# Fewer PE instructions, long fp32 dummies and moved value casts in the head of a linear-attention plus feed-forward kernel

## The chip, the cores and the metric

The kernel runs on one core of a Trainium2 chip. The metric is the device time of one execution in microseconds (us). "Before" is the kernel as it stood, "changed" the kernel with the diff below.

Engine names in the profile: PE is TensorE's matmuls, PEld its weight loads, DVE VectorE, ACT ScalarE, POOL GpSimd, SP the queue that issues most transfers. A "look" is the one profiled execution of a kernel; its times in us count from its first instruction.

## The reference, cut to what matters

```
q, k, v: (8 batches, 8 heads, 576 rows, 64)  f32
q_s = softmax of q over the last axis
k_s = softmax of k over the rows
kv  = k_s^T v            (64 x 64 per head)
x   = q_s kv             -> (4608, 512)
h   = x @ w_in           (512 x 2048)
g   = h * sigmoid(beta * h)
out = g @ w_out          (2048 x 512)
```

## The kernel before: the parts that the change and the argument touch

Heads go in four pairs per batch. In the head of the program (batch 0) each pair of queries is exponentiated, normalised and transposed. The keys are exponentiated, and `kv` is their product with a bf16 copy of the values. The sum over the keys is the product with a column of ones. Then `out_now` multiplies the scaled `kv` with the transposed queries, and a copy from PSUM gives `XT`, the input of the first big product. `WARM` matmuls are dummies.

```
def warm(n, bk):                              # dummies: 512 columns, bf16
    for _ in range(n):
        mm(PS[bk][:, :], WARM[:, 0:128], WARM[:, :], True, True, ...)

def ksum(b, hp, kb):                          # 9 matmuls of one column
    for j in range(NG):
        mm(PS[kb][:, hp:hp + 1], keys, ones, j == 0, j == NG - 1, ...)

def kv_mm(b, hp, bk, n):                      # 9 matmuls of 64 columns
    for j in range(NG):
        mm(PS[bk][:, VW*n : VW*n + D], keys, values[:, 0:D], ...)
...
warm(13, 0) ... warm(6, 0) ... warm(3, 0)     # between the transposes
cast_v(0, 0); cast_v(0, 1, DVE); cast_v(0, 2) # values to bf16; default is POOL
for m in range(NM): cast_win(0, m, 1, POOL)   # w_in, chunk 1
cast_win(1, 0, 2, POOL)                       # w_in, chunk 2, first half
...
ksum(0, 0, kb); ksum(0, 1, kb); ksum_inv(0, kb, 0, 2)
go(t_steps(0, (3,), (1,)))
warm(1, 0); cast_v(0, 3, ACTE)
...
at = first_tiles(0, FIRST[0])                 # hidden tiles 1 and 2
kv_mm(0, 0, 3, 0); kv_mm(0, 1, 3, 1); kvd(0, 0, 3, 0, 2)
ksum(0, 2, kb); ksum(0, 3, kb); warm(1, 0); ksum_inv(0, kb, 2, 2)
beta = read_beta()
kv_mm(0, 2, 5, 0)
out_now(0, 0, 4, ACTE)                        # 1st output product, XT copy on ACT
kv_mm(0, 3, 5, 1)
out_now(0, 1, 6, ACTE)
kvd(0, 2, 5, 0, 2); next(beta); next(beta)
at(0)                                         # first w_in matmuls
out_now(0, 2, 7, DVE); out_now(0, 3, 3, ACTE)
...
cast_win(1, 2, 2, DVE); next(beta)
for m in range(1, NM): at(m)
for c in range(2, len(WCH)):                  # chunks 3, 4, 5 of w_in
    for m in range(NM): cast_win(c, m, 1, DVE)
```

The loads are issued in one queue in this order, and none up to the last chunk of `w_in` waits for an engine: q, k, v of batch 0 (3.3 MB), then `w_in` in chunks of 256, 256, 512, 512 and 512 columns (0.5, 0.5, 1, 1 and 1 MB). Then come `w_out` (4 MB), as staging buffers come free, and q, k, v of batch 1. Hidden tiles 1 to 4 need the first two chunks, tiles 5 to 8 the third, tiles 9 to 12 the fourth. "The fifth tile" below is the first that needs the third chunk, and "PE's head" is all that PE does before it.

The softmax here doesn't subtract the row's maximum and nothing guards it: scores larger than these inputs give would overflow.

## Time and profile before

The time is 287.42 us (median of 3 executions).

| kernel before, one execution | |
|---|---|
| span | 285.5 us |
| PE busy | 278.9 us (98%) |
| third chunk of w_in landed | 19.06 us |
| PE's head ready for the fifth tile | 18.97 us (its last matmul starts at 18.76, one takes 0.216) |
| fifth tile starts | 19.57 us |
| first w_out matmul | 30.30 us |

PE is nearly full over the span. The windows view of the first 20 us shows another bound there. Columns are the stretch, its length, busy time and instruction count of PE, PEld, DVE, ACT and POOL, then the granted clock, the DMA share and GB/s:

```profile
0.00:10.00 10.00, 8.80 (x38) 3.78 (x38) 5.34 (x12) 6.65 (x11) 7.59 (x18) 1.00 0.82 286
10.00:15.00 5.00, 4.27 (x86) 3.30 (x87) 4.05 (x13) 3.67 (x5) 2.85 (x6) 1.00 1.06 373
15.00:20.00 5.00, 4.34 (x20) 1.63 (x18) 2.54 (x9) 4.25 (x8) 0.70 (x2) 1.00 1.05 386
```

From 10 us on the DMA share stays at 1.05 or above, with 373 and 386 GB/s, while every engine has idle time. The chain of work that ended last, in order of time (start, length, what; issue pieces under 0.1 us left out), passes through a transfer:

```profile
8.18 10.88 DMA WST<-in_moe_w_in_dram
19.08 0.44 DVE WIN L572
19.57 20.82 PE PS L363 x94
```

That is the third chunk, cast by DVE, after which PE starts. PE's own timeline (start, length, engine and line, operation, count, and in brackets the idle time before it and what ended it) says how near PE's head was to being the bound:

```profile
13.29 0.43 PE L363 MATMUL PS<-VB,EK 128*128 128x64 bf16 x9
13.56 0.38 PE L363 MATMUL PS<-QT,KVD 128*128 128x512 bf16 x1
13.77 0.43 PE L363 MATMUL PS<-VB,EK 128*128 128x64 bf16 x9
14.05 0.38 PE L363 MATMUL PS<-QT,KVD 128*128 128x512 bf16 x1
14.70 0.59 PE L363 MATMUL PS<-XT,WIN 128*128 128x512 bf16 x2 [0.28 <-POOL WIN L572]
15.13 0.59 PE L363 MATMUL PS<-QT,KVD 128*128 128x512 bf16 x2
15.56 0.59 PE L363 MATMUL PS<-XT,WIN 128*128 128x512 bf16 x2
16.39 2.75 PE L363 MATMUL PS<-XT,WIN 128*128 128x512 bf16 x12 [0.23 <-DVE XT L521]
19.57 10.89 PE L363 MATMUL PS<-XT,WIN 128*128 128x512 bf16 x48 [0.43 <-DVE WIN L572]
```

The sixteen matmuls of tiles 1 to 4 were done 0.43 us before the fifth tile could start. (The view counts the end of a matmul with its drain; by start times the gap is 0.6 us.)

### The profile page before, as it was taken

The page shows a single profiled execution, that of the slowest core. Times are in us where ns is not written, and L with a number is a line of the kernel's source. Part 1 is how long each engine was busy: PE and PEld are TensorE (multiplying, and loading weights), DVE is VectorE, ACT ScalarE, POOL GpSimd, SP SyncE. Part 2 cuts the span into 40 slices and gives each one's busy share as a digit, 9 for nine tenths or more (in the row PEclk, how much of TensorE's full clock was granted, in tenths as well). Part 3 has the DMA queues.
Part 4 walks back from the last instruction along what each step waited for, and adds up shares of the span by engine and source line. Part 5 has one row for each costly group of instructions (what it writes and reads, how often), then busy time and mean ns, then how long its engine had stood idle before and what let it go on. Part 6 is the DMA issues. An engine that isn't in the chain of part 4 may idle for free.

```text
span 285.5 us, 3917 instructions
## 1 busy us (share of the span) xinstructions
PE 278.9 (98%) x1602; PEld 135.5 (47%) x1602; DVE 115.3 (40%) x211; ACT 177.4 (62%) x239; POOL 36.5 (13%) x58
## 2 busy tenths in 40 slices
PE   8989999999999999999999999999999999999994
PEld 3635445444455445544454445444544444444441
DVE  3856696009691248114741563055705200110021
ACT  5878586889977935796479736892650186028500
POOL 7510032305303030300130000000000000000000
PEclk9999999999999999999999999999999999999999
DMA  7999999994899999507960033002600020021022
GB/s 246 378 385 414 384 383 379 331 382 87 247 403 176 390 310 384 66 18 242 374 121 1 2 147 75 2 1 110 131 0 0 37 112 0 0 91 59 0 73 73
DMA packets 41438, 50.07 MB, mean 175 GB/s; under 512 B 20166, under 2 KB 29386, under 8 KB 40140
## 3 DMA queue, kind: packets, MB, share of 16 engines
q1 hardware_dynamic: 40556, 48.77, 54.3%
q10 hardware_dynamic: 864, 1.05, 1.2%
q8 instruction: 12, 0.20, 0.3%
q14 instruction: 6, 0.05, 0.1%
HBM read 36.71 MB, written 9.44 MB: 162 GB/s over the span
## 4 chain that ended last, share of the span: by engine, by line
PE 91%; DMA 4%; SPq 2%; DVE 1%; issue 0%
PE PS L363 91%; DMA WST<-in_moe_w_in_dram 4%; SPq L260 1%; SPq L566 0%; DVE KVD L400 0%; SPq L250 0%; PE PS L361 0%; DVE O2S L713 0%; SPq L533 0%; DVE WIN L572 0%; DVE RC L421 0%
## 5 line engine op out<-in xcount | busy, mean ns | idle before, releaser
L656 ACT ACTIVATE GT<-PS,BETA 128x512 bf16<-128x512 f32 x144 | 97.7, 687 | 78.3 <-PE PS L363 78.2
L363 PE MATMUL PS<-XT,WIN 128*128 128x512 bf16 x576 | 132.7, 379 | 0.9 <-DVE WIN L572 0.4
L363 PE MATMUL PS<-WOUT,GT 128*128 128x512 bf16 x576 | 132.6, 379 | 0.0
L363 PEld LDWEIGHTS PS<-XT,WIN 128*128 128x128 bf16 x576 | 60.1, 106 | 61.0 <-DVE WIN L572 1.6
L363 PEld LDWEIGHTS PS<-WOUT,GT 128*128 128x128 bf16 x576 | 54.4, 98 | 62.7 <-DVE O2S L713 0.2
L713 DVE COPY O2S<-PS 128x512 f32<-128x512 f32 x34 | 23.2, 686 | 110.7 <-PE PS L363 110.7
L363 PE MATMUL PS<-VB,EK 128*128 128x65 bf16 (+2 forms) x324 | 36.4, 190 | 0.0
L349 POOL CAST VB<-VF 128x576 bf16<-128x576 f32 x30 | 21.5, 717 | 73.6 <-DMA VF<-in_v_dram 46.9
L305 ACT ACTIVATE EK<-KF 64x1152 bf16<-64x1152 f32 x24 | 27.8, 1158 | 0.4
L363 PEld LDWEIGHTS PS<-VB,EK 128*128 128x128 bf16 x324 | 22.6, 97 | 7.1 <-issue 0.3
L330 DVE TENSOR_REDUCE QS<-EQ 128x8 f32<-128x512 bf16 (+1 forms) x22 | 20.1, 916 | 3.6 <-ACT EQ L293 3.5
L438 DVE CAST XT<-PS 128x512 bf16<-128x512 f32 x24 | 16.4, 690 | 10.9 <-PE PS L363 10.9
L293 ACT ACTIVATE EQ<-QF 128x512 bf16<-128x512 f32 x32 | 17.9, 619 | 4.1 <-DMA QF<-in_q_dram 3.8
L332 DVE TENSOR_TENSOR EQ<-EQ,QI 128x1024 bf16<-128x1024 bf16 (+1 forms) x16 | 16.8, 1053 | 0.6
L363 PE MATMUL PS<-QT,KVD 128*128 128x512 bf16 x32 | 12.0, 379 | 0.1
L332 POOL TENSOR_TENSOR EQ<-EQ,QI 128x512 bf16<-128x512 bf16 x6 | 6.2, 1042 | 33.8 <-DVE QI L331 33.6
L315 ACT ACTIVATE EK<-KF 64x1152 bf16<-64x1152 f32 (+1 forms) x10 | 9.5, 967 | 1.7 <-DMA KF<-in_k_dram 1.6
L363 PE MATMUL PS<-WARM 128*128 128x512 bf16 x24 | 8.8, 516 | 1.2 <-DVE WARM L221 1.2
L338 DVE TENSOR_REDUCE QRS<-EQR 128x8 f32<-128x512 bf16 x4 | 2.7, 680 | 13.9 <-ACT EQR L320 13.9
L400 DVE TENSOR_TENSOR KVD<-PS,RC 64x128 bf16<-64x128 f32 (+1 forms) x22 | 7.7, 349 | 1.4 <-PE PS L363 0.7
L656 ACT ACT_TABLE_LOAD x5 | 6.4, 1283 | 0.1
L293 ACT ACT_TABLE_LOAD x5 | 6.4, 1283 | 0.1
(48 smaller groups left out, 74.7 us busy)
## 6 DMA issues: line engine op xcount, KB each, us to landing
out_dram<-O2S SPq DMA_DIRECT2D x8, 1024.0 KB, 5.3
KF<-in_k_dram SPq DMA_DIRECT2D x6, 1152.0 KB, 9.5
VF<-in_v_dram SPq DMA_DIRECT2D x6, 1152.0 KB, 12.4
QF<-in_q_dram SPq DMA_DIRECT2D x6, 1024.0 KB, 7.8
KF<-in_k_dram SPq DMA_DIRECT2D x8, 288.0 KB, 7.0
VF<-in_v_dram SPq DMA_DIRECT2D x8, 288.0 KB, 7.3
O2S<-in_moe_w_in_dram SPq DMA_DIRECT2D x2, 1024.0 KB, 13.2
WST<-in_moe_w_out_dram SPq DMA_DIRECT2D x2, 1024.0 KB, 9.7
```

The lines of the kernel that those rows point to most:

```text
L260: add(SP, lambda e, a=a, o=o: e.dma_start(o, a), w=[(name, i, hp) for hp in range(c * n, c * n + n)], slot=f"{name}{i}_{c}")
L293: add(ACTE, lambda e, o=o, a=a: e.activation(o, a, ACT.Exp), r=[("qf", i, hp)], w=[("eq", i, hp)])
L305: add(ACTE, lambda e, o=o, a=a: e.activation(o, a, ACT.Exp), r=[("kf", i, h) for h in hps], w=[("ek", i, h, e_) for h in hps])
L315: add(ACTE, lambda e: e.activation(o, a, ACT.Exp), r=[("kf", i, h) for h in hps], w=[("ek", i, h, e_) for h in hps])
L330: add(DVE, lambda e: e.tensor_reduce(s_, a, AX.X, ALU.add), r=ks, w=[("qs", i, hp0)])
L332: add(eng, lambda e: e.tensor_tensor(a, a, vb, ALU.mult), r=ks + [("qi", i, hp0)], w=ks)
L349: add(eng, lambda e: (e.copy if eng == ACTE else e.tensor_copy)(o, a), r=[("vf", i, h) for h in hps] + [("vone", i)], w=[("vb", i, h) for ...
L363: add(PE, lambda e: e.matmul(o, l, r_, start=start, stop=stop), r=r, w=w, bank=[bk])
L400: add(DVE, lambda e, o=o, a=a, s_=s_: e.tensor_tensor(o, a, s_, ALU.mult), r=[("ps", bk)] + [("rc", i, h) for h in hps], w=[("kvd", i, h, ...
L438: add(eng, lambda e: (e.copy if eng == ACTE else e.tensor_copy)(XT[i][:, hp, :], PS[bk][:, :]), r=[("ps", bk)], w=[("xt", i, hp)], bank=[bk])
L656: add(ACTE, lambda e: e.activation(GT[:, f, :], PS[bk][:, :], ACT.Silu, scale=BETA[:, f:f + 1]), r=[("ps", bk), "beta"], w=[("gt", f)], ba ...
L713: add(eng, lambda e: (e.copy if eng == ACTE else e.tensor_copy)(O2S[t % 2][:, u, :], PS[bk][:, :]), r=[("ps", bk)], w=[("o2", t % 2, u)], ...
```

## The change

Its intent is fewer PE instructions in the head. The key sums of pairs 2 and 3 ride as a 65th column of the kv product, which drops 18 matmuls. Dummies become fewer and longer by reading the same bytes as fp32. The second value cast moves from DVE to POOL, and the fourth is split between ACT (5 of 9 groups) and POOL (4 of 9). The order also changes: the first output product now follows the fourth kv product, and `beta` is read after the third XT copy is queued.

```diff
+        def cast_v(b, hp, eng=POOL, part=None):     # part 0: groups 0-4, part 1: 5-8
 ...
-        def warm(n, bk):
+        def warm(n, bk, long=False):
+            w = WARM[:, :].bitcast(F32) if long else WARM
             for _ in range(n):
-                mm(PS[bk][:, :], WARM[:, 0:128], WARM[:, :], True, True, r=["warm"],
+                mm(PS[bk][:, 0:256] if long else PS[bk][:, :], w[:, 0:128], w[:, :], True, True,
 ...
-        def kv_mm(b, hp, bk, n):
+        def kv_mm(b, hp, bk, n, w=D):               # w = D + 1 takes the ones column along
 ...
-        warm(13, 0)
+        warm(6, 0, True)
 ...
-        warm(6, 0)
+        warm(3, 0, True)
 ...
-        warm(3, 0)
+        warm(1, 0, True)
 ...
-        cast_v(0, 1, DVE)
+        cast_v(0, 1)
         cast_v(0, 2)
+        cast_v(0, 3, POOL, 1)
 ...
-        ksum_inv(0, kb, 0, 2)
+        ksum_inv(0, kb, 0, 2, 0, 1)
+        warm(2, 0)
         go(t_steps(0, (3,), (1,)))
-        warm(1, 0)
-        cast_v(0, 3, ACTE)
+        cast_v(0, 3, ACTE, 0)
 ...
-        ksum(0, 2, kb)
-        ksum(0, 3, kb)
-        warm(1, 0)
-        ksum_inv(0, kb, 2, 2)
-        beta = read_beta()
-        kv_mm(0, 2, 5, 0)
+        kv_mm(0, 2, 5, 0, D + 1)
+        kv_mm(0, 3, 5, 1, D + 1)
         out_now(0, 0, 4, ACTE)
-        kv_mm(0, 3, 5, 1)
         out_now(0, 1, 6, ACTE)
+        ksum_inv(0, 5, 2, 2, D, VW)
         kvd(0, 2, 5, 0, 2)
-        next(beta)
-        next(beta)
         at(0)
         out_now(0, 2, 7, DVE)
         out_now(0, 3, 3, ACTE)
+        beta = read_beta()
+        next(beta)
+        next(beta)
```

More of the change, by code (lines that the diff above doesn't have):

```diff
@@ L342, in norm_rem @@
                 r=[("eqr", i), "qri"], w=[("eqr", i)])
-        def cast_v(b, hp, eng=POOL, n=1):
+        def cast_v(b, hp, eng=POOL, part=None):
             i = b % 2
-            hps = range(hp, hp + n)
-            o = bass.AP(VB[i], hp * NG * VW, [[NHP * NG * VW, 128], [VW, NG * n], [1, 64]])
-            a = bass.AP(VF[i], hp * KW, [[NHP * KW, 128], [64, NG * n], [1, 64]])
+            j0, n = ((0, NG), (0, 5), (5, 4))[0 if part is None else part + 1]
+            o = bass.AP(VB[i], (hp * NG + j0) * VW, [[NHP * NG * VW, 128], [VW, n], [1, 64]])
+            a = bass.AP(VF[i], hp * KW + j0 * D, [[NHP * KW, 128], [64, n], [1, 64]])
             add(eng, lambda e: (e.copy if eng == ACTE else e.tensor_copy)(o, a),
-                r=[("vf", i, h) for h in hps] + [("vone", i)], w=[("vb", i, h) for h in hps])
+                r=[("vf", i, hp), ("vone", i)],
+                w=[("vb", i, hp, h) for h in ((0, 1) if part is None else (part,))])
         rot = [0]
@@ L389, in kv_rows @@
                     [("ek", i, hp, 0), ("ek", i, hp, 1), ("ekz", i, 0), ("ekz", i, 1)],
-                    [("vb", i, hp)], [("vone", i)])
+                    [("vb", i, hp, 0), ("vb", i, hp, 1)], [("vone", i)])
         def kvd(b, hp, bk, c, n=1):
@@ L492, in spread @@
             return [(lo + (hi - lo) * k / len(steps), s) for k, s in enumerate(steps)]
-        def warm(n, bk):
+        def warm(n, bk, long=False):
+            w = WARM[:, :].bitcast(F32) if long else WARM
             for _ in range(n):
-                mm(PS[bk][:, :], WARM[:, 0:128], WARM[:, :], True, True, r=["warm"],
-                   w=[("ps", bk)], bk=bk)
+                mm(PS[bk][:, 0:256] if long else PS[bk][:, :], w[:, 0:128], w[:, :], True, True,
+                   r=["warm"], w=[("ps", bk)], bk=bk)
         def ksum(b, hp, kb):
@@ L505, in ksum, with ksum_inv @@
                    w=[("ps", kb)], bk=kb)
-        def ksum_inv(b, kb, hp0, n):
+        def ksum_inv(b, kb, hp0, n, c0, step):
             i = b % 2
-            add(DVE, lambda e: e.reciprocal(RC[i][:, hp0:hp0 + n], PS[kb][:, hp0:hp0 + n]),
+            s_ = bass.AP(PS[kb], c0, [[512, 128], [step, n]])
+            add(DVE, lambda e: e.reciprocal(RC[i][:, hp0:hp0 + n], s_),
                 r=[("ps", kb)], w=[("rc", i, hp) for hp in range(hp0, hp0 + n)], bank=[kb])
-        def kv_mm(b, hp, bk, n):
+        def kv_mm(b, hp, bk, n, w=D):
             for j in range(NG):
                 l, r_, ke, kv, ko = kv_rows(b, hp, j)
-                mm(PS[bk][:, VW * n:VW * n + D], l, r_[:, 0:D], j == 0, j == NG - 1,
-                   r=ke + kv, w=[("ps", bk)], bk=bk)
+                mm(PS[bk][:, VW * n:VW * n + w], l, r_[:, 0:w], j == 0, j == NG - 1,
+                   r=ke + kv + ko, w=[("ps", bk)], bk=bk)
         def out_now(b, hp, bk, eng):
```

## The prediction

> **What bounds it now.** PE is 98% busy (278.9 of 285.5 us, table of engines). In the head, in the chain of waits in order of time, everything before 19.57 us is the load queue issuing (0.75 to 8.18 us) and then one piece of 10.88 us, the transfer of the third chunk of w_in (columns 512 to 1023), landing at 19.06; DVE casts its first quarter (0.44 us), and at 19.57 PE starts the fifth hidden tile. From there PE has almost no gap. The windows show DMA saturated (share 0.82 up to 10 us, then 1.05, 370 to 400 GB/s); no load up to that chunk waits for an engine. So the time is about "landing of the third chunk plus 268 us of PE", and PE's own head (up to the first 16 w_in matmuls) already ends 0.43 us too early (timeline of PE: idle before 19.57).
>
> **What the change does, all before 19.57 us.**
> - Dummies: 24 bf16 ones (13 at 0.43 us apart, cold, the later ones at 0.22) become 10 fp32 ones of 256 columns and 2 bf16 ones. I estimate an fp32 one at two old ones, as the diff's 13 to 6 implies: the first block takes 5.1 instead of 5.5 us, and the transposes after it wait for data until about 6.4 us anyway.
> - The 18 one-column matmuls of pairs 2 and 3 go (about 0.65 us of PE); the sums ride as a 65th column at no cost.
> - DVE loses a 0.74 us cast at 11.32 and has beta read later; POOL gains that cast (0.66) and 4/9 of the fourth (0.3); ACT's 0.67 cast shrinks to about 0.4. POOL idles 0.85 us before the second value pair and before w_in, so its casts of w_in still start with the data at 13.23.
>
> I expect kv, XT and the first 16 w_in matmuls to end 0.5 to 1.3 us earlier, near 18.2 us (before: about 19.1).
>
> **How much is on the critical path.** None of it: PE then waits longer for the third chunk. Its arrival depends on bytes queued ahead of it and the DMA rate, which the change doesn't touch; the w_out loads, released by the w_in casts, are issued a little earlier than 16.66 us but queue behind 2 MB of w_in. Expected gain 0 to 0.2 us.
>
> **Risk of a cold clock.** The Trainium skill, "TensorE: Matmul & The Clock Gate", Part 1, says the PE runs at half rate until one window of about 3.4 us has been busy and falls back after an idle one. This trace agrees with the start (dummies 0.43 us apart to 6.3 us, 0.22 from 7.0). The longer gap before 19.57, some 1.5 us, is under that window, so PE should stay fast. If the fp32 dummies did not count as busy, the 16 first matmuls would take some 3.5 us more and the time rise by about 2 us, still under 1%.
>
> **Prediction: 287.3 us, 286.7 to 288.0; faster by over 2%: 1%; within 2%: 98%; slower by over 2%: 1%.**
>
> **What would show it.** Right: third chunk still lands at 19.0 to 19.2 us, the fifth hidden tile starts at 19.5 to 19.7, idle before it grows from 0.43 to 1 to 2 us; from 19.6 us on both traces agree within 0.2 us. Wrong: the fifth tile starts much earlier (then DMA was not the floor), or matmuls 0.43 us apart after 8 us (cold clock), or POOL's w_in casts start after 13.5 us.
>
> **What would make it wrong.** A cold clock at the restart, or a later landing through a changed order of transfers.

## The result, and the profile after

The changed kernel took 287.46 us (median of 4: 286.56 to 287.68), the kernel before 287.47 us (median of 4). The ratio is 0.9995 with a 95% interval of 0.997 to 1.0019, so the two are the same.

The one profiled execution was the fastest of the four (286.56 us). The same windows view for the changed kernel:

```profile
0.00:10.00 10.00, 7.83 (x36) 5.95 (x37) 5.36 (x12) 6.47 (x11) 7.58 (x18) 1.00 0.83 285
10.00:15.00 5.00, 3.82 (x66) 2.59 (x67) 3.54 (x10) 3.53 (x5) 3.97 (x8) 1.00 1.07 373
15.00:20.00 5.00, 4.56 (x22) 1.97 (x22) 3.05 (x10) 4.25 (x8) 0.91 (x2) 1.00 1.05 387
```

PE has 0.45 us less recorded work between 10 and 15 us and POOL 1.1 us more. The DMA columns did not move. PE's timeline of the changed kernel:

```profile
12.83 0.99 PE L364 MATMUL PS<-VB,EK 128*128 128x65 bf16 x18 [0.35 <-POOL VB L349]
13.66 0.59 PE L364 MATMUL PS<-QT,KVD 128*128 128x512 bf16 x2
14.80 0.59 PE L364 MATMUL PS<-XT,WIN 128*128 128x512 bf16 x2 [0.55 <-ACT XT L524]
15.23 0.59 PE L364 MATMUL PS<-QT,KVD 128*128 128x512 bf16 x2
15.66 0.60 PE L364 MATMUL PS<-XT,WIN 128*128 128x512 bf16 x2
16.70 12.89 PE L364 MATMUL PS<-XT,WIN 128*128 128x512 bf16 x58 [0.44 <-DVE BC L595]
```

Two things are to be seen. First, the w_in matmuls start at 14.80 us where they started at 14.70 before, so PE's head is no shorter. The freed time stands in the brackets as new waits, 0.35 us for a value cast on POOL and 0.55 us for an XT copy on ACT. Single matmul records are missing in this trace, so the 16.70 is read with care; by weight loads the third step began at 16.46 against 16.36 before.

Second, in this execution the fifth tile did not wait at all. The third chunk happened to land at 18.18 us instead of 19.06, and the tile's first weight load is at 18.86, 0.70 us ahead of the kernel before. At the first w_out weight load of the next 512 rows PE was still 0.77 us ahead (60.34 against 61.11), so this early landing, followed by slightly earlier ones, accounts for the 0.7 us by which this execution's span is shorter than the profiled one of before (284.8 against 285.5).

POOL's timeline shows where the first wait comes from. Before:

```profile
10.19 0.66 POOL L349 CAST VB<-VF 128x576 bf16<-128x576 f32 x1 [0.80 <-DMA VF<-in_v_dram]
11.71 0.67 POOL L349 CAST VB<-VF 128x576 bf16<-128x576 f32 x1 [0.85 <-DMA VF<-in_v_dram]
13.23 1.86 POOL L572 CAST WIN<-WST 128x256 bf16<-128x256 f32 x4 [0.85 <-DMA WST<-in_moe_w_in_dram]
```

After:

```profile
10.24 3.07 POOL L349 CAST VB<-VF 128x576 bf16<-128x576 f32 x4 [0.71 <-DMA VF<-in_v_dram]
13.44 1.86 POOL L575 CAST WIN<-WST 128x256 bf16<-128x256 f32 x4
```

POOL now does three and a half casts in a row. By single records the third value was ready at 12.78 us against 12.38 before, and the last part of the fourth at 13.31 against 13.10. The Trainium skill, "GPSIMD Engine Reference", section 8, says that POOL shares its SBUF interfaces with VectorE and contends with DVE instructions that have two SBUF inputs. This trace agrees: POOL's second cast, which began while DVE's query scaling (two SBUF inputs) ran, took 0.94 us where the other whole ones took 0.66. The first cast ran beside the same scaling and still took 0.66, but the scaling itself took 1.18 us, against 0.98 before and 0.69 for the scaling before it.

### The profile page after: what moved, and what is told of

Same layout as the page of the kernel before. It is cut to its first block, busy times and chain, and to the rows that moved or that the text cites. A ratio compares the mean times of both kernels' runs of the same rounds, so it can differ in the third digit from the quotient of the medians.

```text
span 284.8 us, 3851 instructions
## 1 busy us (share of the span) xinstructions
PE 275.5 (97%) x1551; PEld 137.1 (48%) x1582; DVE 114.9 (40%) x210; ACT 177.0 (62%) x239; POOL 37.4 (13%) x60
## 3 DMA queue, kind: packets, MB, share of 16 engines
q10 hardware_dynamic: 864, 1.05, 1.1%
## 4 chain that ended last, share of the span: by engine, by line
PE 84%; DMA 8%; SPq 3%; DVE 2%; issue 1%; ACT 1%
PE PS L364 84%; DMA O2S<-in_moe_w_in_dram 5%; DMA O2S<-in_moe_w_out_dram 3%; SPq L260 1%; SPq L569 1%; DVE WOUT L553 1%; DVE QS L330 0%; DVE WIN L575 0%; ACT O2S L714 0%; PE PS L362 0%; SPq L250 0%; DVE O2S L714 0%; DVE EQ L332 0%; ACT GT L660 0%; SPq L536 0%
## 5 line engine op out<-in xcount | busy, mean ns | idle before, releaser
L364 PE MATMUL PS<-XT,WIN 128*128 128x512 bf16 x561 | 130.7, 380 | 1.4 <-ACT XT L524 0.6
L364 PE MATMUL PS<-WOUT,GT 128*128 128x512 bf16 x561 | 131.2, 379 | 0.7
L349 POOL CAST VB<-VF 128x576 bf16<-128x576 f32 (+1 forms) x32 | 22.4, 699 | 73.5 <-PE PS L364 60.4
L364 PE MATMUL PS<-WARM 128*128 128x256 f32 (+1 forms) x21 | 7.1, 486 | 1.3 <-DVE WARM L221 1.2
## 6 DMA issues: line engine op xcount, KB each, us to landing
KF<-in_k_dram SPq DMA_DIRECT2D x8, 288.0 KB, 7.1
VF<-in_v_dram SPq DMA_DIRECT2D x8, 288.0 KB, 7.7
```

The source lines that it names most:

```text
L349: add(eng, lambda e: (e.copy if eng == ACTE else e.tensor_copy)(o, a), r=[("vf", i, hp), ("vone", i)], w=[("vb", i, hp, h) for h in ((0, 1 ...
L364: add(PE, lambda e: e.matmul(o, l, r_, start=start, stop=stop), r=r, w=w, bank=[bk])
```

## The experiments

Two theories stood after the result.

- **Floors and an unshortened head.** PE waits for a train of transfers (third chunk, fourth chunk, loads of batch 1), and PE's head is about as long after the change as before.
- **The rival.** The change shortened PE's head by 0.5 to 1.3 us, as predicted, and the landing of the third chunk hid it.

Each set below ran on another chip, with the kernel before in the same rounds.

### First set: a second look, and the third chunk in two pieces

`after_again` is the changed kernel, unedited.

> The changed kernel once more, unedited. Theory L (landing): the time is max(third chunk of w_in landed and cast, PE's head done) plus a constant, and the landing scatters from execution to execution; so here too the time is within 0.3% of the kernel before, and in the profile the fifth hidden tile starts 0.4 to 0.5 us after the landing or at 18.9 us, whichever is later. The early landing of the first look (18.2 us against 19.1 before) was chance: expected here 18.2 to 19.2. Rival C (the change itself makes the transfers land earlier): landing again at 18.2 +- 0.2 and a time 0.2 to 0.3% under before. Either way the first 16 w_in matmuls end near 18.9 us, as before the change, not near 18.2.

Measured: 287.53 us (287.30 to 287.76), ratio 1.0007 (0.9995 to 1.002) to before. The landing was back at 19.05 us. The chain and the PE timeline of this execution:

```profile
8.23 10.82 DMA WST<-in_moe_w_in_dram
19.07 0.44 DVE WIN L575
19.56 8.73 PE PS L364 x38
```

```profile
14.60 0.59 PE L364 MATMUL PS<-XT,WIN 128*128 128x512 bf16 x2 [0.55 <-ACT XT L524]
...
19.56 10.89 PE L364 MATMUL PS<-XT,WIN 128*128 128x512 bf16 x47 [0.52 <-DVE WIN L575]
```

The chain is that of the kernel before to within 0.02 us. The early landing was not a property of the change: two executions of the same code landed at 18.18 and 19.05. Why the landing moves is open. The next chunk's cast began at 21.57 and 21.79, so by then nearly the same had been delivered.

The next two load the third chunk as two loads of 256 columns, in the kernel before and in the changed one.

```diff
-    WCH = ((0, 256), (256, 256), (512, 512), (1024, 512), (1536, 512))
+    WCH = ((0, 256), (256, 256), (512, 256), (768, 256), (1024, 512), (1536, 512))
```

> Kernel before, third chunk of w_in (columns 512 to 1023) loaded as two loads of 256 columns, so the first half should land some 1.3 us earlier (0.5 MB at 390 GB/s). Theory L: the fifth tile no longer waits for a transfer, starts when PE's head is done, about 19.0 instead of 19.57, and the time falls by 0.4 to 0.7 us (0.15 to 0.25%). If the landing alone bound the time (PE's head having slack), it would fall by 1.2 us or more. If the landing were not a bound at all: 0.

> The same split on the changed kernel. Theory L with the head no shorter (H): the fifth tile starts at about 19.0 us as in the split kernel before, the two split kernels agree within 0.2 us. Rival S (the change did shorten PE's head and the landing hid it, as predicted): the fifth tile starts 0.5 to 1.3 us earlier than in the split kernel before, and the time is lower by as much.

`before_split` took 287.22 us, ratio 0.9999 (0.9987 to 1.0012), and `after_split` 287.38 us, ratio 1.0003 (0.9989 to 1.0016). Neither gained, so the expected 0.4 to 0.7 us missed. PE's timeline of `before_split` says why:

```profile
16.32 6.20 PE L363 MATMUL PS<-XT,WIN 128*128 128x512 bf16 x28 [0.23 <-DVE XT L521]
22.76 7.37 PE L363 MATMUL PS<-XT,WIN 128*128 128x512 bf16 x31 [0.24 <-DVE WIN L572]
```

The wait at 19.57 is gone, and a new one stands at 22.76, for the fourth chunk, whose casts began at 22.18. PE had earned 0.88 us at the fifth tile (first weight load 18.69 against 19.57). At the first w_out weight load 0.33 us was left of it (29.75 against 30.08). At the second batch's kv products, near 43 us, it was 0.09 us, because the transposes of batch 1 now waited for their queries too (a block of eight took 0.85 us against 0.61). The landing at 19.06 is one floor of several.

In `after_split` this execution ran late from the first value on (it landed at 10.31 us, against 10.07 in `before_split`), and the fifth tile started at 19.14. The two split kernels agree in time within what these runs resolve, and the changed one shows no shorter head.

`after_best` combines the split with a reordered head on the changed kernel.

```diff
-        cast_v(0, 1)
+        cast_v(0, 1, DVE)
-        kv_mm(0, 3, 5, 1, D + 1)
         out_now(0, 0, 4, ACTE)
+        kv_mm(0, 3, 5, 1, D + 1)
         out_now(0, 1, 6, ACTE)
 ...   beta read ahead of at(0); second chunk loaded in two halves of rows
-        for m in range(1, NM):
-            at(m)
+        at(1); tiles 3 and 4, steps 0 and 1; at(2); at(3); tiles 3 and 4, steps 2 and 3
```

> Changed kernel with the split, with the second chunk loaded in two halves too, with the second value cast on DVE again, the first output matmul ahead of the fourth kv product, beta read before the third XT copy, and hidden tiles 2 and 3 fed their first two contraction steps while the last two XT copies are made. Theory: PE's head ends near 18.3 us and the fifth tile follows at once: 1.0 to 1.4 us (0.35 to 0.5%) under the kernel before. If PE's head were not on the critical path once the landing is out of the way: no better than the split alone.

Measured: 287.27 us, ratio 0.9997 (0.9985 to 1.001). The fifth tile's first weight load came at 18.52, 1.05 us earlier than before, but the ninth tile's was only 0.6 us earlier (22.57 against 23.18), and the time did not change measurably. The expectation missed for the same reason as the split's.

### Second set: the same kernels with the floors taken away

To see PE's head without the transfers, the "light" kernels give wrong results. They load half of the third, fourth and fifth chunk and use it twice, and they do not load w_out. Every engine executes the same compute instructions.

```diff
-        for c in range(1, len(WCH)):
-            load_win(c)
+        load_win(1)
+        for c in range(2, len(WCH)):
+            load_win(c, 0, 2)
 ...   casts and scaling read rows m % 2 and f % 2
-        for c in range(4):
-            load_wout(c)
```

> Wrong result on purpose. Kernel before with only half of the third, fourth and fifth chunk of w_in loaded (each half used twice) and no load of w_out at all (its scaling reads what lies in the staging buffers): same work on every engine, 5.5 MB less to move after the second chunk. Theory F (a train of transfer floors: third chunk, fourth chunk, loads of batch 1): all those floors lie before PE now, PE's head alone sets when the fifth tile starts, 19.0 us, and nothing stalls after: 0.5 to 0.8 us (0.2 to 0.3%) under the kernel before. If the floors were not transfers: no change.

> Wrong result on purpose: the same cut of transfers in the changed kernel. H (the change left the length of PE's head as it was, since its last links are the casts of the values and the XT copies): fifth tile at 18.9 to 19.2 us and a time within 0.2 us of the light kernel before. S (the head did get shorter by 0.5 to 1.3 us, and only the transfers hid it): 0.5 us or more under the light kernel before.

> Wrong result on purpose: the same cut of transfers in the changed kernel with the head reordered (second value cast on DVE, first output matmul ahead of the fourth kv product, beta read earlier, tiles 2 and 3 started during the last XT copies). F: with the transfers out of the way a shorter head is worth its full length: fifth tile at 18.2 to 18.6 us, 0.4 to 0.7 us under the light kernel before, where with all transfers in place the same reordering gave 0.03%. Rival: something after the head absorbs it here too, no difference between the light kernels.

| kernel | median us | ratio to before (95%) | fifth tile, first weight load | first w_out weight load |
|---|---|---|---|---|
| before (first look) | 287.42 | 1 | 19.57 | 30.08 |
| before_light | 286.39 | 0.9968 (0.9955 to 0.998) | 18.80 | 29.16 |
| after_light | 286.44 | 0.9967 (0.9954 to 0.9979) | 18.65 | 29.01 |
| best_light | 286.00 | 0.9953 (0.9941 to 0.9966) | 18.18 | 28.54 |

The last lines of PE's head, kernel before_light, then after_light, then best_light. The window ended at 24 us, so these lines run past the fifth tile:

```profile
16.43 7.93 PE L363 MATMUL PS<-XT,WIN 128*128 128x512 bf16 x36 [0.23 <-DVE XT L521]
```

```profile
16.28 7.93 PE L364 MATMUL PS<-XT,WIN 128*128 128x512 bf16 x36 [0.23 <-DVE BC L591]
```

```profile
15.05 9.11 PE L364 MATMUL PS<-XT,WIN 128*128 128x512 bf16 x40
```

No wait for a chunk is left in any of the three. The floors were worth 0.9 us (0.32%), a little more than the 0.5 to 0.8 expected. With them gone the changed kernel is still no faster than the kernel before, and its head ends 0.15 us earlier in one look each. **The rival falls**: by the five times of each there was no hidden gain of 0.5 us or more. The reordered kernel's ratio is lower than before_light's by 0.0015 (0.4 us), which was expected, though the intervals overlap.

The looks alone would not carry this, because the loads of the values land at other times in each. The fourth value landed at 12.85 us in before_light, 12.23 in after_light and 11.99 in best_light. From that landing to the last of the 16 weight loads of tiles 1 to 4 it is 5.74, 6.20 and 5.97 us. So the earlier ends of the two changed heads in the table are not shown to be the work of the code. With all transfers in place the same stretch is 6.14 us in the kernel before and in before_split, and 6.18 and 6.21 in the two looks at the changed kernel: no shorter either. In after_best and in after_best2 (below) it is 5.64 and 5.66, so by this measure the reordered head is shorter.

`after_best2` was an attempt at a faster kernel with the right result. It has the reordered head, and the second, third and fourth chunks loaded in two halves of rows. Batch 1's transposes come two matmuls later and its remainder outputs four matmuls later.

```diff
-            load_win(c)
+            for m in (0, 2) if c in (1, 2, 3) else (0,):
+                load_win(c, m, 2 if c in (1, 2, 3) else NM)
-        TT = (110, 120)
+        TT = (112, 120)
-                todo = spread(outr_steps(1), 97, 101) + attn_late(2)
+                todo = spread(outr_steps(1), 101, 105) + attn_late(2)
 ...   and the reordered head of after_best
```

> An attempt at a faster kernel with a right result: reordered head, second, third and fourth chunk loaded in two halves of contraction rows (pieces as long as before, unlike the split by columns), transposes of batch 1 two matmuls later, remainder outputs of batch 1 four matmuls later. F: fifth tile near 18.4, eighth tile no stall over 0.2 us, 0.4 to 0.9 us (0.15 to 0.3%) under the kernel before; if the next transfer takes it all again, 0.

Measured: correct, 286.79 us (286.67 to 286.95), ratio 0.9981 (0.9967 to 0.9994). Which of its edits gave the gain was not separated. All five runs are faster than all nine of before in the same rounds (287.16 to 287.75). PE's timeline has no gap from the second pair of w_in matmuls on, and the next floor shows further down the chain:

```profile
15.53 13.58 PE L364 MATMUL PS<-XT,WIN 128*128 128x512 bf16 x62
...
39.89 0.40 PE L362 MATMUL PS<-IDB,EQ 128*128 128x128 bf16 x4 [0.20 <-POOL EQ L332]
```

```profile
32.84 8.51 DMA VF<-in_v_dram
...
41.40 1.07 POOL VB L349
```

Of the 1.35 us that PE was ahead at the first w_out weight load (28.73 against 30.08), 0.64 us was left at the first w_out weight load of the next 512 rows (60.47 against 61.11), and 0.6 us in the median time. The lines above show one of the waits in between, 0.2 us for a query scaling of batch 1, and a transfer of batch 1's values that the chain now runs through. This is the fastest right kernel.

### Third set: which part of the change did what to the head

All four are light kernels, compared with the light kernels of the second set. Those ran on another chip, so the ratios to the kernel before of the same rounds are safer than the medians.

```diff
  after_order_light: the changed kernel with the old order
-        kv_mm(0, 3, 5, 1, D + 1)
         out_now(0, 0, 4, ACTE)
+        kv_mm(0, 3, 5, 1, D + 1)
```

> Wrong result on purpose (the cut transfers of the light kernels, as for all four of this set). Light changed kernel with one edit: the first output matmul goes ahead of the fourth kv product again, as in the kernel before. Theory O (PE's freed time was spent waiting: the changed order hangs the first XT copy on the last value cast): first XT copy done 0.3 to 0.5 us earlier, head shorter by 0.1 to 0.4 us and the time 0.1 to 0.4 us under the light changed kernel (286.44). If order does not matter: within 0.1 us.

Measured: 285.95 us, ratio 0.9946 (0.9933 to 0.9958), against 0.9967 for after_light. That is 0.5 us by the medians and 0.6 us by the ratios, somewhat more than the 0.1 to 0.4 expected. The intervals just overlap. The traces agree with it:

```profile
13.18 0.39 PE L364 MATMUL PS<-QT,KVD 128*128 128x512 bf16 x1
...
14.34 0.59 PE L364 MATMUL PS<-XT,WIN 128*128 128x512 bf16 x2 [0.27 <-POOL WIN L575]
...
16.05 8.14 PE L364 MATMUL PS<-XT,WIN 128*128 128x512 bf16 x37 [0.23 <-POOL WIN L575]
```

The first output product starts at 13.18 (13.45 in after_light) and the first w_in matmul at 14.34 (14.59), although the first value's cast began 0.17 us later in this execution. From that cast to the first w_in matmul it is 4.14 us against 4.56. From the landing of the fourth value to the last weight load of tiles 1 to 4 it is 5.80 us against 6.20. So the moved product cost about 0.4 us of head. It had hung the first XT copies behind the last value cast.

The ratio is also below that of before_light (0.9968), by about 0.6 us. So the rest of the change may be worth something with the old order. The head does not show it (5.80 us against 5.74), the two intervals touch, and no light kernel before ran in these rounds, so this stays open.

`after_oldcasts_light` keeps the new order and all else, and puts the casts back.

```diff
-        cast_v(0, 1)
+        cast_v(0, 1, DVE)
         cast_v(0, 2)
-        cast_v(0, 3, POOL, 1)
-        cast_v(0, 3, ACTE, 0)
+        cast_v(0, 3, ACTE)
```

> Light changed kernel with the casts of the values put back as before (second on DVE, fourth whole on ACT); fewer key sums, long dummies and the new order stay. Theory P (GpSimd doing three and a half casts in a row delays the third and fourth): third value ready 0.3 to 0.4 us earlier and the third kv product starts at once after the second, but with the first output matmul still behind the fourth product the head shortens by less, 0 to 0.3 us. If the casts were what cost the gain, the head shortens by 0.5 us or more.

Measured: 286.36 us, ratio 0.9956 (0.9944 to 0.9967). The third and fourth kv product:

```profile
12.56 0.46 PE L364 MATMUL PS<-VB,EK 128*128 128x65 bf16 x9 [0.26 <-DVE QT L382]
13.29 0.46 PE L364 MATMUL PS<-VB,EK 128*128 128x65 bf16 x9 [0.27 <-ACT VB L349]
```

Against the expectation the third did not start at once: PE waited 0.26 us for a DVE copy, and then 0.27 us for the fourth value, now cast on ACT. So POOL's row of casts was only part of why PE waited. From the first cast to the first w_in matmul it is 4.41 us against 4.56. The casts cost the head about 0.15 us in this look (0.17 from the fourth value's landing), less than the order did. In time the difference to after_light (286.44, ratio 0.9967) is within the noise.

`casts_light` is the light kernel before with the moved casts alone.

> Light kernel before with the moved casts alone (second on GpSimd, fourth split over ACT and GpSimd). P: third and fourth value ready 0.2 to 0.4 us later, but PE is then still in the key sums, so the head grows by 0 to 0.2 us: within 0.2 us of the light kernel before (286.39), not faster.

Measured: 286.91 us, ratio 0.9975 (0.9958 to 0.9992), and six runs in two groups: 286.16, 286.19 and 286.46 at a mean granted clock of 0.999 to 1.0, and 287.35, 287.44 and 287.50 at 0.992 to 0.994. The first group agrees with before_light (286.16 to 286.97), so by it the casts alone cost nothing, as expected. The second group was not expected. The profiled execution belongs to it, and its windows show what happened (the third number from the end is the granted clock):

```profile
8.00:10.00 2.00, 1.74 (x16) 1.15 (x15) 1.90 (x6) 1.98 (x4) 1.40 (x2) 1.00 1.03 395
10.00:12.00 2.00, 1.60 (x27) 1.33 (x28) 1.80 (x5) 1.98 (x2) 1.61 (x2) 0.90 1.05 391
12.00:14.00 2.00, 2.00 (x39) 1.62 (x38) 0.98 (x4) 0.65 (x2) 1.67 (x4) 0.50 1.07 356
14.00:16.00 2.00, 1.74 (x22) 1.14 (x21) 0.64 (x3) 0.88 (x2) 1.63 (x4) 0.75 1.06 374
```

The PE clock fell to one half from about 11.6 to 15.0 us (worked out from the 0.90 and 0.75), just while the kv products ran. The fifth tile started 1.1 us later (19.91 against 18.80), and that group's mean is 1.2 us longer. The lowered clock is in the executions and not only in this trace: a mean of 0.994 over 285.5 us is 0.006 x 285.5 / 0.5 = 3.4 us at half clock.

With this mark the other runs can be counted. Of the 45 executions of kernels with the short bf16 dummies whose clock is on record (29 of the kernel before, 5 before_split, 5 before_light, 6 casts_light), 11 have a mean of 0.994 or less. Of 44 of kernels with the long ones (9 of the changed kernel and 35 of its variants, without nodum_light) there are 2, both of after_split. The long dummies come with the rest of the change in all of these, so which part keeps the clock up is not separated. Where the dip lies in an unprofiled execution is not known either. In the kernel before it costs nothing that these runs can see: its 7 executions with a dip average 287.44 us, its 22 without 287.45.

`nodum_light` is the light changed kernel without any dummy.

> Light changed kernel without any dummy matmuls, to see what they are for. If they keep the clock up: the kv products and the first w_in matmuls come 0.43 us apart[...], the 16 first w_in matmuls end 1 to 3 us later and the time rises by as much. If the transposes and key sums were enough to raise the clock: no change.

Measured: 287.31 us (286.68 to 288.47), ratio 0.9994 (0.9976 to 1.0012), above after_light by 0.9 us in the medians and 0.8 us by the ratios. PE's timeline:

```profile
15.16 1.01 PE L364 MATMUL PS<-XT,WIN 128*128 128x512 bf16 x2 [0.34 <-ACT XT L524]
15.96 1.01 PE L364 MATMUL PS<-QT,KVD 128*128 128x512 bf16 x2
16.81 2.55 PE L364 MATMUL PS<-XT,WIN 128*128 128x512 bf16 x10
```

Pairs of 512-column matmuls take 1.01 us up to 16.8 us, where they take 0.59 with dummies, and the head ends 1.2 us later (19.84 against 18.65). So the dummies do keep the clock up, and they are worth 0.8 to 0.9 us when no transfer hides it. The long dummies alone, and the ones column alone, were not run.

## Why the prediction was right or wrong

- **The time and the class: right.** Predicted 287.3 us (286.7 to 288.0), "within 2%" at 98%; measured 287.46 us, ratio 0.9995. This does not vouch for the steps before the floor: behind a landing at 19.06 us the time comes out the same whether PE's head ends at 18.2 us or at 18.9.
- **The third chunk's landing as the floor: right, and too small a part.** The chain of before and of after_again goes through it (19.06 and 19.05 us). Taking it away alone gained nothing, since the fourth chunk and batch 1's loads stand behind it. With these gone too the kernel before fell by 0.9 us. The scatter of the landing (18.18 in one look) was not foreseen either. "Lands at 19.0 to 19.2" failed in that look, and with it the fifth tile at 19.5 to 19.7 (18.86) and the agreement within 0.2 us after it (first w_out weight load 29.22 against 30.08). All three held in after_again.
- **"I expect kv, XT and the first 16 w_in matmuls to end 0.5 to 1.3 us earlier, near 18.2 us": this step failed.** With the floors away the times were equal (286.44 and 286.39 us). PE's head ended at 18.65 us against 18.80, with the fourth value landing 0.62 us earlier. The mistake was to count removed PE work as a shorter head: PE waited for the values and the XT copies instead. The wait before the fifth tile did not grow to 1 to 2 us either: it was 0.52 in after_again and absent in the first look.
- **Where that gain went.** The 18 one-column matmuls did go, but the third and fourth value casts became ready later on POOL, and PE waited 0.35 us there. With the old casts it still waited 0.26 and 0.27 us. The first output product was put behind the fourth kv product, so PE waited 0.55 us for its XT copy. Undoing the order alone shortened this stretch by about 0.4 us, undoing the casts alone by about 0.15.
- **POOL's w_in casts "still start with the data": right in effect.** They began at 13.44 and 13.24 us, against 13.23. What I had not costed is POOL's serial casting between 10.2 and 13.3.
- **w_out's first load "a little earlier than 16.66 us": wrong.** It was issued at 17.27, because beta's reads now stand between the third XT copy and the cast that frees the buffer. No cost of it shows: the two chunks queued ahead of it landed at 21.55 and 24.25 us.
- **An fp32 dummy at two old ones: right.** The six of the first block appear as 12 matmul records 0.43 us apart, while the clock is low. The Trainium skill, "FP8 and Floating Point Precision", TensorE Precision Notes, says true fp32 takes four passes through the array: 256 columns x 4 is the time of two 512-column bf16 matmuls, which agrees.
- **The cold clock: right for the changed kernel as profiled, incomplete as a mechanism.** It rose at about 4.7 us and stayed up. But a fall needs no 3.4 us of idle PE, as casts_light showed.

## What to carry to other kernels

Work removed from an engine in a stretch that ends in a transfer's landing is worth nothing until the landing moves. Here moving one landing uncovered the next, so list all of them down the queue before costing a gain. Removing instructions from the fullest engine shortens a chain only if that engine is what the chain waits for: check who feeds its next instruction, and don't pay for the removal with a later cast or a worse order. To find out whether a change had a hidden gain, take the hiding transfers away in both kernels and compare those. Compare by times of several runs, or measure from the landing that feeds the stretch, because landings move from execution to execution.

## What the Trainium skill lacked or had wrong

- "TensorE: Matmul & The Clock Gate", Part 1 has the clock fall back after an idle window. In casts_light it fell for 3.4 us (the window's length agrees) with PE busy 1.74 and 1.60 of 2.00 us in the two stretches from 8 to 12 us, and no wait of PE there over 0.4 us in the timeline. The same part also has the clock fall where PE idles briefly and often between groups of matmuls, so the page is incomplete here and not contradicted. That stretch was mostly transposes and one-column matmuls. Part 4 says that transposes don't count as busy in the same way. No page says how much short matmuls count, and no run here separates it.
- No page says that the granted clock of a profile can read 1.00 from the start while PE is still at half rate. In nodum_light it reads 1.00 from 14 to 16 us while pairs of matmuls take 1.01 us instead of 0.59, and in the kernel before while the first dummies are 0.43 us apart. This is the view and not the chip: the trace's record of the clock begins only at the rise (16.79 us in nodum_light, 6.90 in the kernel before), and the time without a record is shown as 1.00. The mean clocks above leave that start out too.
- No page says that a profile shows one fp32 matmul as two weight loads and two matmuls (12 records for 6 dummies). Fewer instructions in the code were not fewer in the array.
- No page gives the scatter of a queued transfer's landing. The 1 MB load of the third chunk landed at 19.06, 18.18 and 19.05 us in three executions, while the casts of the next chunk began within 0.22 us of one another.
